# Attention kernel on one Trainium2 core: four heads of one batch per step, with the query projected in column tiles

## The chip, the cores and the metric

The kernel runs on one core of a Trainium2 chip. The metric is the device time of one execution in microseconds (us). A run is called slow when it is over 1.5% above the fastest of the same kernel, otherwise fast. Medians are of all runs on record; of the runs quoted here only one is slow, in experiment 1, and it is left out of the ratio. Ratios are the mean time of one kernel's fast runs over that of the other's in the same rounds on the same chip, so they are not quite the ratio of the medians that are quoted too.

Words used below: **PE** is TensorE's matmul row of the profile and **PEld** its weight loads; **DVE** is VectorE, **ACT** ScalarE, **POOL** GpSimd, **SP** the engine that issues the DMAs. A **step** handles four (batch, head) pairs of problem B, 128 query rows in all; there are 128 steps.

## The reference

Two attention blocks with cached keys and values, A with 4 key/value heads for 32 query heads, B with 32 for 32; their outputs stand side by side. The change touches B alone:

```python
# B, Sq, D = 16, 32, 1024;  H, Sk, Dh = 32, 1024, 128;  all bf16
q = (x @ wq).reshape(B, Sq, H, Dh).transpose(0, 2, 1, 3)
scores = einsum("bhqd,bhkd->bhqk", q, k_cache) * Dh ** -0.5
p = softmax(scores)
o = einsum("bhqk,bhkd->bhqd", p, v_cache)
return o.transpose(0, 2, 1, 3).reshape(B, Sq, H * Dh) @ wo
```

B's keys and values are 134 MB each, so the kernel is a stream of cache loads with work for every engine behind it.

## The kernel before

The program records its operations, and a list scheduler with a table of durations sets the order on each engine at build time. The parts that matter here are B's query projection, the shuffle that brings the query to where the scores need it, the key load and the scores.

```python
# projection of 128 tokens (4 batches) for 4 heads: 8 matmuls of 128x512
for j in range(j0, j0 + JS):
    last = e.matmul(ps_pj[:, 0:CW], xT_sb[:, 1, j, G * P:(G + 1) * P], wq_sb[:, 1, j, :],
                    start=(j == 0), stop=(j == DJ - 1))
# ... copied to Qtok (partition = batch, query), DVE-transposed in 32x32 blocks to QBt
# the shuffle: 16 matmuls with the identity and 4 ACT copies a group
for rg in range(4):
    last = e.matmul(QSH[0][32 * rg:32 * rg + 32, 0:2 * Dh]..., ident[32 * a:32 * a + 32, ...], rhs,
                    start=True, stop=True, tile_position=(32 * a, 32 * rg))
...
evac(QR[:, gp, a, :, :], QSH[0][:, 0:2 * Dh]..., name="QR_ev", eng="act", ...)

# keys: 2 batches x 2 heads a step, 2 runs of 16 keys (4 KB) per partition
ksrc = pb["k"][q.b0:q.b0 + 2, q.h0:q.h0 + 2].rearrange("t hh (p s) d -> (hh p) t (s d)", s=16)
pr.add("sp", lambda e: e.dma_start(KB_sb[:, sl, :, :], ksrc), ...)
# ... DVE transposes KB_sb in 32x32 blocks to KBt_sb; scores are 32 matmuls of 32x32 tiles, 512 columns;
# one exp of 1024 columns with a row sum; 4 transposes of P; 32 column-tiled matmuls with V
```

The key buffer has two slots. A slot is free for the next load when the DVE transposes have read it, and these write KBt_sb, which is free when TensorE's scores have read it.

## Time and profile before

The kernel before takes 917.8 us (median of 4 runs, 911.66 to 923.61). The profile is of one more run, of 913.31 us.

| What | Value | Where |
|---|---|---|
| hardware DMA queue busy | 97.6% | page, part 3 |
| DMA rate, mean / best slices | 375 / 409 to 411 GB/s | page, part 2 |
| PE busy | 86% | page, part 1 |
| DMA rate over 100 to 880 us | 388 GB/s | windows |

DMA is the resource that is nearly full, and TensorE follows.

The groups of instructions, kept apart by shape (busy us, mean ns | idle time of the engine before them and who ended it), show the costs that the change removes or alters.

```profile
L848 DVE STREAM_TRANSPOSE KBt_sb<-KB_sb 128x1024 f32<-128x1024 f32 x256 | 306.6, 1223 | 46.3 <-DMA KB_sb<-in_B_k_cache_dram 22.6 <-PE ps_s L887 18.9 <-PE ps_o L971 2.4
L887 PE MATMUL ps_s<-KBt_sb,QR 32*32 32x512 bf16 x4096 | 167.0, 402 | 13.8 <-ACT P_sb L907 7.4 <-DVE KBt_sb L848 4.4 <-ACT QR L588 1.2
...
L907 ACT ACTIVATE P_sb<-ps_s 128x1024 bf16<-128x1024 f32 x128 | 131.7, 1029 | 70.3 <-PE ps_pt L921 36.5 <-PE ps_s L887 28.1 <-DVE KBt_sb L848 2.0
...
L921 PE MATMUL ps_pt<-id,P_sb 128*128 128x128 f32 x512 | 91.7, 302 | 18.4 <-ACT P_sb L907 16.9 <-ACT PT_sb L588 1.3
...
L674 PE MATMUL ps_pj<-wq_sb,xT_sb 128*128 128x512 bf16 x256 | 71.0, 391 | 4.3 <-ACT QR L588 1.8 <-ACT xT_sb L588 1.2 <-DMA wq_sb<-in_B_wq_dram 0.6
...
L588 ACT CAST QR<-ps_pj 128x256 bf16<-128x256 f32 x128 | 48.5, 379 | 46.0 <-PE ps_pj L694 43.3 <-PE ps_s L887 2.6
...
L694 PE MATMUL ps_pj<-QBt,ident 32*32 32x256 bf16 x512 | 43.9, 287 | 17.5 <-ACT QR L588 10.0 <-DVE acc L748 2.6 <-DVE Qtok L590 1.5
...
```

The shuffle is L694 on PE and the QR copies on ACT. The key transposes (L848) are the biggest item on DVE; they wait 18.9 us in all for scores (L887) to free KBt_sb.

The waits of SP, which issues the loads (total us, times, longest), and the windows of the start and the middle (stretch, its length, busy us and instructions of PE, PEld, DVE, ACT and POOL, then granted clock, DMA share, GB/s):

```profile
SPq L813 <- DVE KBt_sb L848: 220.4, 64, 13.0
...
```
```profile
0.00:100.00 100.00, 77.32 (x800) 37.64 (x800) 34.88 (x56) 34.78 (x58) 6.45 (x16) 0.86 0.85 308
100.00:880.00 780.00, 687.02 (x11461) 386.27 (x11454) 472.01 (x809) 418.24 (x774) 61.38 (x59) 0.98 1.01 388
...
```

SP waits for DVE's key transposes before it can load the next keys. At 410 GB/s, the best slices, the 341.64 MB would need about 833 us by estimate; the rest is lost at the start, at the end and in such holes.

### The profile page before, as it was taken

The page shows a single profiled execution, that of the slowest core. Times are in us where ns is not written, and L with a number is a line of the kernel's source. Part 1 is how long each engine was busy: PE and PEld are TensorE (multiplying, and loading weights), DVE is VectorE, ACT ScalarE, POOL GpSimd, SP SyncE. Part 2 cuts the span into 40 slices and gives each one's busy share as a digit, 9 for nine tenths or more (in the row PEclk, how much of TensorE's full clock was granted, in tenths as well). Part 3 has the DMA queues.
Part 4 walks back from the last instruction along what each step waited for, and adds up shares of the span by engine and source line. Part 5 has one row for each costly group of instructions (what it writes and reads, how often), then busy time and mean ns, then how long its engine had stood idle before and what let it go on. Part 6 is the DMA issues. An engine that isn't in the chain of part 4 may idle for free.

```text
span 911.5 us, 28186 instructions
## 1 busy us (share of the span) xinstructions
PE 783.4 (86%) x12610; PEld 432.9 (47%) x12610; DVE 519.3 (57%) x891; ACT 462.1 (51%) x853; POOL 67.9 (7%) x76
## 2 busy tenths in 40 slices
PE   5879999999998899988898789989897888978775
PEld 2325564545554454545454455536453445545332
DVE  1415655466645566555756556666665656666553
ACT  2215665655564455655564555555554544646242
POOL 0000000100110010101010010001010100001000
PEclk7879999999999999999999999999999899989898
DMA  9789899999999999999999999999999999899995
GB/s 333 270 302 370 308 399 361 402 385 390 359 380 409 411 349 400 401 381 392 368 405 403 411 374 390 375 346 397 405 408 399 385 398 403 333 409 397 385 410 190
DMA packets 151934, 341.64 MB, mean 375 GB/s; under 512 B 10496, under 2 KB 26880, under 8 KB 151808
## 3 DMA queue, kind: packets, MB, share of 16 engines
q1 hardware_dynamic: 151808, 339.78, 97.6%
q8 instruction: 101, 1.65, 0.7%
q14 instruction: 25, 0.20, 0.1%
HBM read 337.64 MB, written 2.10 MB: 373 GB/s over the span
## 4 chain that ended last, share of the span: by engine, by line
PE 56%; ACT 14%; DVE 13%; DMA 12%; issue 2%; SPq 2%; POOL 0%; POOLq 0%; DVEq 0%; ACTq 0%
PE ps_pj L735 10%; PE ps_s L887 10%; DVE KBt_sb L848 6%; PE ps_o L971 6%; PE ps_pj L657 6%; PE ps_pt L921 6%; ACT P_sb L907 5%; PE ps_pj L674 5%; PE ps_kt L937 4%; DMA KB_sb<-in_B_k_cache_dram 4%; ACT PTA_sb L901 3%; PE ps_s L865 3%; DMA wq_sb<-in_A_wq_dram 3%; DVE acc L748 3%; PE ps_kt L839 2%
## 5 line engine op out<-in xcount | busy, mean ns | idle before, releaser
L848 DVE STREAM_TRANSPOSE KBt_sb<-KB_sb 128x1024 f32<-128x1024 f32 x256 | 306.6, 1223 | 46.3 <-DMA KB_sb<-in_B_k_cache_dram 22.6
L887 PE MATMUL ps_s<-KBt_sb,QR 32*32 32x512 bf16 x4096 | 167.0, 402 | 13.8 <-ACT P_sb L907 7.4
L901 ACT ACTIVATE PTA_sb<-ps_s 128x1024 bf16<-128x1024 f32 x128 | 131.6, 1029 | 73.1 <-PE ps_s L865 59.9
L907 ACT ACTIVATE P_sb<-ps_s 128x1024 bf16<-128x1024 f32 x128 | 131.7, 1029 | 70.3 <-PE ps_pt L921 36.5
L588 ACT COPY PT_sb<-ps_pt 128x512 f32<-128x512 f32 x128 | 74.9, 585 | 150.6 <-PE ps_o L971 116.5
L822 POOL COPY VAp_sb<-VA_sb 128x1024 bf16<-128x1024 bf16 x64 | 66.6, 1040 | 770.5 <-DMA VA_sb<-in_A_v_cache_dram 667.3
L921 PE MATMUL ps_pt<-id,P_sb 128*128 128x128 f32 x512 | 91.7, 302 | 18.4 <-ACT P_sb L907 16.9
L987 DVE TENSOR_SCALAR OB_sb<-ps_o,rinv_all 128x128 bf16<-128x128 f32 x128 | 44.4, 347 | 108.0 <-PE ps_o L971 107.6
L921 PEld LDWEIGHTS ps_pt<-id,P_sb 128*128 128x128 f32 x512 | 74.2, 208 | 43.2 <-ACT P_sb L907 25.2
L971 PE MATMUL ps_o<-VB_sb,PT_sb 128*32 128x128 bf16 x4096 | 84.9, 224 | 8.4 <-DMA VB_sb<-in_B_v_cache_dram 6.7
L865 PE MATMUL ps_s<-QT_sb,KTA_sb 128*128 128x256 bf16 x512 | 85.3, 275 | 4.2 <-ACT PTA_sb L901 2.2
L735 PE MATMUL ps_pj<-woB_sb,OTB_sb 128*128 128x512 bf16 x256 | 75.4, 391 | 12.9 <-DVE acc L748 5.4
L937 PE MATMUL ps_kt<-VAp_sb,PTA_sb 128*128 128x129 bf16 x1024 | 80.3, 221 | 5.4 <-ACT KTA_sb L588 2.3
L971 PEld LDWEIGHTS ps_o<-VB_sb,PT_sb 128*32 128x32 bf16 x4096 | 60.1, 98 | 52.1 <-issue 38.7
L657 PE MATMUL ps_pj<-xT_sb,wq_sb 128*128 128x512 bf16 x256 | 74.0, 406 | 11.4 <-DMA wq_sb<-in_A_wq_dram 4.2
L887 PEld LDWEIGHTS ps_s<-KBt_sb,QR 32*32 32x32 bf16 x4096 | 49.7, 90 | 67.5 <-issue 19.5
L937 PEld LDWEIGHTS ps_kt<-VAp_sb,PTA_sb 128*128 128x128 bf16 x1024 | 64.9, 98 | 31.2 <-issue 13.4
L674 PE MATMUL ps_pj<-wq_sb,xT_sb 128*128 128x512 bf16 x256 | 71.0, 391 | 4.3 <-ACT QR L588 1.8
L735 PE MATMUL ps_pj<-woA_sb,OTA_sb 128*128 128x512 bf16 x256 | 66.9, 389 | 7.4 <-DVE ost L751 4.7
L588 ACT CAST QR<-ps_pj 128x256 bf16<-128x256 f32 x128 | 48.5, 379 | 46.0 <-PE ps_pj L694 43.3
L748 DVE TENSOR_TENSOR acc<-acc,ps_pj 128x512 f32<-128x512 f32 x64 | 43.5, 680 | 44.6 <-PE ps_pj L735 44.2
L865 PEld LDWEIGHTS ps_s<-QT_sb,KTA_sb 128*128 128x128 bf16 x512 | 44.3, 98 | 32.3 <-ACT PTA_sb L901 5.8
(52 smaller groups left out, 574.0 us busy)
## 6 DMA issues: line engine op xcount, KB each, us to landing
KB_sb<-in_B_k_cache_dram SPq DMA_DIRECT2D x128, 1024.0 KB, 8.2
VB_sb<-in_B_v_cache_dram SPq DMA_DIRECT2D x256, 512.0 KB, 8.9
KA_sb<-in_A_k_cache_dram SPq DMA_DIRECT2D x64, 256.0 KB, 9.5
VA_sb<-in_A_v_cache_dram SPq DMA_DIRECT2D x64, 256.0 KB, 7.7
wq_sb<-in_B_wq_dram SPq DMA_DIRECT2D x32, 256.0 KB, 6.9
wq_sb<-in_A_wq_dram SPq DMA_DIRECT2D x32, 256.0 KB, 8.7
woB_sb<-in_B_wo_dram SPq DMA_DIRECT2D x32, 256.0 KB, 8.4
woA_sb<-in_A_wo_dram SPq DMA_DIRECT2D x32, 256.0 KB, 7.8
```

The costliest lines, as they stand in the source:

```text
L588: pr.add("act", lambda e: e.copy(dst_ap, src_ap), reads=reads, writes=writes, name=name + "@act", wtag=wtag, rtag=rtag)
L657: last = e.matmul(ps_pj[:, 0:tn], wq_sb[:, 0, j, hc * Dh:(hc + 1) * Dh], xT_sb[:, 0, j, t0:t0 + tn], start=(j == 0), stop=(j == DJ - 1))
L674: last = e.matmul(ps_pj[:, 0:CW], xT_sb[:, 1, j, G * P:(G + 1) * P], wq_sb[:, 1, j, :], start=(j == 0), stop=(j == DJ - 1))
L735: last = e.matmul(ps_pj[:, 0:OUTW], OT[:, gp, hh, :], wo_[:, hh, oh * OUTW:(oh + 1) * OUTW], start=(hh == 0), stop=(hh == nh - 1))
L848: pr.add("dve", lambda e: e.transpose(KBt_sb[:, sl, t_, :].bitcast(F32), KB_sb[:, rs, t_, :].bitcast(F32)), reads=[("KB", rs)], writes=[(" ...
L865: last = e.matmul(ps_s[:, sbf, c2, i * 2 * P:(i + 1) * 2 * P], KTA_sb[:, sl, c * P:(c + 1) * P], qt, start=True, stop=True)
L887: last = e.matmul(ps_s[32 * cg:32 * cg + 32, sbf, g2, :].rearrange("p (s j) -> p s j", s=16), lhsT, rhs, start=(fp == 0), stop=(fp == 3), ...
L901: pr.add("act", lambda e: e.activation(dst, src, ACTF.Exp, scale=scale), writes=BK_S[sbf] + [("PTA", q.half)], name="expA", rtag={("Sv", s ...
L907: pr.add("act", lambda e: e.activation(dst, src, ACTF.Exp, scale=scale, accum_out=stat[:, 0:1]), writes=BK_S[sbf] + ["P", "rowsum"], name= ...
L921: last = e.transpose(ps_pt32[:, m * P:(m + 1) * P], p32[:, m:Sk // 2:NPK], id32[:])
L937: last = e.matmul(ps_kt[:, qh * OA0:qh * OA0 + Dh + 1], PTA_sb[:, h, c, qh * P:(qh + 1) * P], VAp_sb[:, sl, 4 * h + c, 0:Dh + 1], start=(h ...
L971: last = e.matmul(ps_o[32 * a:32 * a + 32, 0:Dh], PT_pairs[:, c // 2, 32 * a:32 * a + 32, c % 2], VB_sb[:, kvs, a // 2, a % 2, c, :], star ...
```

## The change

A step now takes four heads of one batch. Each head gets a quadrant of 32 partitions, each partition 32 keys in one run of 8 KB. The intent is to halve the number of key packets and to have no shuffle: the projection is written so that a head's query comes out in its own quadrant, which takes column tiles of 32 columns. So that the eight matmuls of a round of scores use eight different tiles of the array, as before (there 32 of them took 1.14 us together in the timeline, where the mean of one is 402 ns), half of a head's scores land in another quadrant (`a ^ 2`); therefore the exp is cut in two, and two small DVE adds bring the halves of a row sum together.

```diff
-                ksrc = pb["k"][q.b0:q.b0 + 2, q.h0:q.h0 + 2].rearrange("t hh (p s) d -> (hh p) t (s d)", s=16)
+                ksrc = pb["k"][q.b, q.h0:q.h0 + 4].rearrange("a (p s) d -> (a p) (s d)", s=32)
 ...  (projection, per group of 128 tokens)
-                        last = e.matmul(ps_pj[:, 0:CW], xT_sb[:, 1, j, G * P:(G + 1) * P], wq_sb[:, 1, j, :], start=(j == 0), stop=(j == DJ - 1))
+            for bq in range(4):
+                    for j in range(DJ):
+                        for hh in range(4):
+                            last = e.matmul(ps_pj[32 * hh:32 * hh + 32, bq * Dh:(bq + 1) * Dh],
+                                            xT_sb[:, 1, j, G * P + 32 * bq:G * P + 32 * bq + 32], wq_sb[:, 1, j, hh * Dh:(hh + 1) * Dh],
+                                            start=(j == 0), stop=(j == DJ - 1), tile_position=(0, 32 * hh))
 ...
-        def qprepB_sh(m_, G, a_list):      # the shuffle, 16 matmuls and 4 copies a group: removed
 ...  (scores)
+                            cg = a ^ (2 * g)
+                            last = e.matmul(ps_s[32 * cg:32 * cg + 32, sbf, g, :]..., lhsT, kt[32 * a:32 * a + 32, g, :, :, o0:o0 + 63:2],
+                                            start=(fp == 0), stop=(fp == 3), tile_position=(32 * a, 32 * cg))
 ...  (exp)
+                for g in range(2):
+                    pr.add("act", lambda e, ...: e.activation(dst, src, ACTF.Exp, scale=scale, accum_out=st[:, g:g + 1]), ... name="exp", ...)
+                for i in range(2):
+                    o, r = 64 * i, 64 * (1 - i)
+                    pr.add("dve", lambda e, ...: e.tensor_tensor(st[o:o + 64, 2:3], st[o:o + 64, 0:1], st[r:r + 64, 1:2], ALU.add), ... name="shift", ...)
 ...  (the transposes of P in two halves; V by heads; output by heads)
```

More of the change, by code (lines that the diff above doesn't have):

```diff
@@ L18 @@
 LAZY_DELAY = 0
-QSH_IN_PJ = True
 A_STEPS_FRAC = 0.92
@@ L26 @@
 PRIO_BONUS = {}
-PE_MODE = {"scoresB": 2, "Qshuf": 2, "PVB": 1}
+PE_MODE = {"scoresB": 2, "PVB": 1, "qprojB": 1}
 MODE_SWITCH = 0.11
@@ L31 @@
     "scoresB": 1.1, "scoresA": 0.45, "PT_trB": 0.50, "PVB": 0.8, "OT_tr": 0.10, "KTA_tr": 0.50,
-    "Qshuf": 0.25, "qprojA": 1.8, "qprojB": 1.8, "oprojA": 1.8, "oprojB": 0.9, "xT_tr": 0.5,
-    "exp": 1.25, "expA": 1.05, "VAp_cp": 1.2, "normA@dve": 0.42, "OT_trA": 0.2, "OT_evA@dve": 0.35, "PT_ev@act": 0.52, "norm@act": 0.46, "OT_ev@act": 0.24, "KTA_ev@act": 0.93, "qA_ev@act": 0.52, "qB_ev@act": 0.52,
-    "QR_ev@act": 0.31, "acc0": 0.52, "xT_ev@act": 0.93, "o_fin@act": 0.52,
+    "qprojA": 1.8, "qprojB": 1.8, "oprojA": 1.8, "oprojB": 0.9, "xT_tr": 0.5,
+    "exp": 0.82, "shift": 0.12, "expA": 1.05, "VAp_cp": 1.2, "normA@dve": 0.42, "OT_trA": 0.2, "OT_evA@dve": 0.35, "PT_ev@act": 0.52, "norm@act": 0.46, "OT_ev@act": 0.24, "KTA_ev@act": 0.93, "qA_ev@act": 0.52, "qB_ev@act": 0.52,
+    "acc0": 0.52, "xT_ev@act": 0.93, "o_fin@act": 0.52,
     "KBt_tr": 1.15, "recip": 0.15, "norm@dve": 0.30, "PT_ev@dve": 0.62, "OT_ev@dve": 0.16, "KTA_ev@dve": 0.62,
     "QBt_tr": 0.35, "acc+": 0.62, "accF": 0.62, "qA_ev@dve": 0.62, "qB_ev@dve": 0.62, "xT_ev@dve": 0.62, "o_fin@dve": 0.62,
-    "QR_ev@dve": 0.35,
     "c0": 0.2, "c1": 0.3,
@@ L531, in build @@
         z32 = sb("z32", [P, P], F32)
-        stat = sb("stat", [P, 4], F32)
+        stat = sb("stat", [P, 2, 4], F32)
         rinv_all = sb("rinv_all", [P, 2 * NIT], F32)
@@ L540, in build @@
         Qtok = sb("Qtok", [P, 2, NG, CW], BF)
-        QBt = sb("QBt", [P, CW], BF)
-        QR = sb("QR", [P, 2, 4, 2, Dh], BF)
+        QBt = sb("QBt", [P, 2, CW], BF)
         woA_sb = sb("woA_sb", [P, HS, D], BF)
@@ L549, in build @@
         KBt_sb = sb("KBt_sb", [P, 2, 2, 16 * Dh], BF)
-        VB_sb = sb("VB_sb", [P, NVB, 2, 2, NCH, Dh], BF)
+        VB_sb = sb("VB_sb", [P, NVB, 4, NCH, Dh], BF)
         KA_sb = sb("KA_sb", [P, 2, NCH, Dh], BF)
@@ L569, in build @@
         BK_KT, BK_PT, BK_O, BK_PJ = ("bank", 4), ("bank", 5), ("bank", 6), ("bank", 7)
-        QSH = (ps_pj, BK_PJ) if QSH_IN_PJ else (ps_kt, BK_KT)
         pr.add("pool", lambda g: g.memset(zeros[:], 0.0), writes=["zeros"], name="c0")
@@ L667, in qprojB, with e_qp @@
             lazy_flush(("wq", 1, m_))
-            JS = 2 if DJ % 2 == 0 else 1
-            for j0 in range(0, DJ, JS):
-                def e_qp(e, j0=j0):
+            for bq in range(4):
+                def e_qp(e, bq=bq):
                     last = None
-                    for j in range(j0, j0 + JS):
-                        last = e.matmul(ps_pj[:, 0:CW], xT_sb[:, 1, j, G * P:(G + 1) * P], wq_sb[:, 1, j, :], start=(j == 0), stop=(j == DJ - 1))
-                    return last
-                pcs = sorted(set(j * WQP // DJ for j in range(j0, j0 + JS)))
-                pr.add("pe", e_qp, reads=[("wq", 1, k_) for k_ in pcs] + [("xT", 1, G)], writes=[BK_PJ], name="qprojB", dur=0.225 * JS,
-                       rtag=dict((("wq", 1, k_), m_) for k_ in pcs))
+                    for j in range(DJ):
[3 more added lines that the diff above has]
+                                            start=(j == 0), stop=(j == DJ - 1), tile_position=(0, 32 * hh))
+                    return last
+                pr.add("pe", e_qp, reads=[("wq", 1, k_) for k_ in range(WQP)] + [("xT", 1, G)], writes=[BK_PJ], name="qprojB", dur=0.45,
+                       rtag=dict((("wq", 1, k_), m_) for k_ in range(WQP)))
@@ L679, in qprojB, with qprepB @@
             evac(Qtok[:, m_ % 2, G, :], ps_pj[:, 0:CW], reads=[BK_PJ], writes=[BK_PJ, ("Qtok", m_ % 2, G)], name="qB_ev",
                  wtag={("Qtok", m_ % 2, G): m_})
-        def qprepB_tr(m_, G):
-            pr.add("dve", lambda e: e.transpose(QBt[:, :].bitcast(F32), Qtok[:, m_ % 2, G, :].bitcast(F32)),
-                   reads=[("Qtok", m_ % 2, G)], writes=["QBt"], name="QBt_tr", rtag={("Qtok", m_ % 2, G): m_}, wtag={"QBt": (m_, G)})
-        def qprepB_sh(m_, G, a_list):
+        def qprepB(m_, G):
@@ L687, in qprepB_sh @@
             gp = (m_ * NG + G) % 2
-            for a in a_list:
-                def e_sh(e, a=a):
-                    last = None
-                    for rg in range(4):
-                        e_ = rg // 2
-                        rhs = QBt[32 * a:32 * a + 32, :].rearrange("p (hp e x) -> p e hp x", hp=2, e=2)[:, e_, :, :]
-                        last = e.matmul(QSH[0][32 * rg:32 * rg + 32, 0:2 * Dh].rearrange("p (hp x) -> p hp x", hp=2),
-                                        ident[32 * a:32 * a + 32, 32 * a:32 * a + 32], rhs, start=True, stop=True,
-                                        tile_position=(32 * a, 32 * rg))
-                    return last
-                pr.add("pe", e_sh, reads=["QBt", "ident"], writes=[QSH[1]], name="Qshuf", rtag={"QBt": (m_, G)})
-                evac(QR[:, gp, a, :, :], QSH[0][:, 0:2 * Dh].rearrange("p (hp x) -> p hp x", hp=2), reads=[QSH[1]],
-                     writes=[QSH[1], ("QR", gp, a)], name="QR_ev", eng="act", wtag={("QR", gp, a): (m_, G)})
+            pr.add("dve", lambda e: e.transpose(QBt[:, gp, :].bitcast(F32), Qtok[:, m_ % 2, G, :].bitcast(F32)),
+                   reads=[("Qtok", m_ % 2, G)], writes=[("QBt", gp)], name="QBt_tr", rtag={("Qtok", m_ % 2, G): m_}, wtag={("QBt", gp): (m_, G)})
@@ L785, in mk_quadB @@
             q.G = (t // 4) % NG
-            jb = t % 4
-            q.bp = jb // 2
-            q.hp = jb % 2
-            q.b0 = 4 * q.G + 2 * q.bp
-            q.h0 = q.m * MS + 2 * q.hp
+            q.bq = t % 4
+            q.b = 4 * q.G + q.bq
+            q.h0 = q.m * MS
             q.kvslot = t % 2
@@ L795, in mk_quadB @@
             q.sbuf = None
-            q.first_of_group = (jb == 0)
-            q.last_of_group = (jb == 3)
+            q.first_of_group = (q.bq == 0)
+            q.last_of_group = (q.bq == 3)
             q.qid = ("B", t)
@@ L811, in st_dmaK @@
                 sl = q.krslot
-                ksrc = pb["k"][q.b0:q.b0 + 2, q.h0:q.h0 + 2].rearrange("t hh (p s) d -> (hh p) t (s d)", s=16)
-                pr.add("sp", lambda e: e.dma_start(KB_sb[:, sl, :, :], ksrc), writes=[("KB", sl)], dma_key=f"kb{sl}", name="kb_dma", dur=4 * Sk * Dh * 2, wtag={("KB", sl): q.kid})
+                ksrc = pb["k"][q.b, q.h0:q.h0 + 4].rearrange("a (p s) d -> (a p) (s d)", s=32)
+                pr.add("sp", lambda e: e.dma_start(KB_sb[:, sl, :, :].rearrange("p i n -> p (i n)"), ksrc), writes=[("KB", sl)], dma_key=f"kb{sl}", name="kb_dma", dur=4 * Sk * Dh * 2, wtag={("KB", sl): q.kid})
         def st_dmaV(q):
@@ L826, in st_dmaV @@
                 for t_ in range(2):
-                    vsrc = pb["v"][q.b0 + t_, q.h0:q.h0 + 2].rearrange("hh (p c) d -> p hh c d", c=NCH)
-                    pr.add("sp", lambda e, t_=t_, vsrc=vsrc: e.dma_start(VB_sb[:, sl, t_, :, :, :], vsrc), writes=[("VB", sl, t_)],
+                    vsrc = pb["v"][q.b, q.h0 + 2 * t_:q.h0 + 2 * t_ + 2].rearrange("a (p c) d -> p a c d", c=NCH)
+                    pr.add("sp", lambda e, t_=t_, vsrc=vsrc: e.dma_start(VB_sb[:, sl, 2 * t_:2 * t_ + 2, :, :], vsrc), writes=[("VB", sl, t_)],
                            dma_key=f"vb{sl}_{t_}", name="vb_dma", dur=2 * Sk * Dh * 2, wtag={("VB", sl, t_): q.kid})
@@ L872, in st_scores @@
                 gp = (q.m * NG + q.G) % 2
+                kt = KBt_sb[:, sl, :, :].rearrange("p i (s x) -> p (i s) x", s=16).rearrange("p (sh g cl) x -> p g sh cl x", g=2, cl=4)
                 def e_s(e, fp):
                     last = None
-                    if True:
-                        f, pd = fp // 2, fp % 2
-                        o0 = f * 64 + pd
-                        for t_ in range(2):
-                            a = 2 * q.bp + t_
-                            for hh in range(2):
-                                cg = 2 * t_ + hh
-                                for g2 in range(2):
-                                    rg = 2 * hh + g2
-                                    lhsT = QR[32 * rg:32 * rg + 32, gp, a, q.hp, o0:o0 + 63:2]
-                                    rhs = KBt_sb[32 * rg:32 * rg + 32, sl, t_, :].rearrange("p (s x) -> p s x", s=16)[:, :, o0:o0 + 63:2]
-                                    last = e.matmul(ps_s[32 * cg:32 * cg + 32, sbf, g2, :].rearrange("p (s j) -> p s j", s=16), lhsT, rhs,
-                                                    start=(fp == 0), stop=(fp == 3), tile_position=(32 * rg, 32 * cg))
+                    f, pd = fp // 2, fp % 2
+                    o0 = f * 64 + pd
+                    for a in range(4):
+                        lhsT = QBt[32 * a:32 * a + 32, gp, q.bq * Dh + o0:q.bq * Dh + o0 + 63:2]
+                        for g in range(2):
+                            cg = a ^ (2 * g)
+                            last = e.matmul(ps_s[32 * cg:32 * cg + 32, sbf, g, :].rearrange("p (sh cl j) -> p sh cl j", sh=4, cl=4), lhsT,
+                                            kt[32 * a:32 * a + 32, g, :, :, o0:o0 + 63:2],
+                                            start=(fp == 0), stop=(fp == 3), tile_position=(32 * a, 32 * cg))
@@ L889, in e_s @@
                     return last
                 for fp_ in range(4):
-                    pr.add("pe", lambda e, fp_=fp_: e_s(e, fp_), reads=[("QR", gp, 2 * q.bp), ("QR", gp, 2 * q.bp + 1), ("KBt", sl, 0), ("KBt", sl, 1)],
+                    pr.add("pe", lambda e, fp_=fp_: e_s(e, fp_), reads=[("QBt", gp), ("KBt", sl, 0), ("KBt", sl, 1)],
                            writes=BK_S[sbf], name="scoresB", dur=0.275, tag="B%d" % q.t,
-                           rtag={("QR", gp, 2 * q.bp): (q.m, q.G), ("QR", gp, 2 * q.bp + 1): (q.m, q.G), ("KBt", sl, 0): q.kid, ("KBt", sl, 1): q.kid},
+                           rtag={("QBt", gp): (q.m, q.G), ("KBt", sl, 0): q.kid, ("KBt", sl, 1): q.kid},
@@ L904, in st_exp @@
             else:
-                src = ps_s[:, sbf, :, :].rearrange("p g (s j) -> p g j s", s=16)
-                dst = P_sb[:, :].rearrange("p (g j s) -> p g j s", g=2, s=16)
-                pr.add("act", lambda e: e.activation(dst, src, ACTF.Exp, scale=scale, accum_out=stat[:, 0:1]),
-                       writes=BK_S[sbf] + ["P", "rowsum"], name="exp",
-                       rtag={("Sv", sbf): q.qid}, wtag={"P": q.qid, "rowsum": q.qid})
+                st = stat[:, q.t % 2, :]
+                for g in range(2):
+                    src = ps_s[:, sbf, g, :].rearrange("p (sh cl j) -> p j sh cl", sh=4, cl=4)
+                    dst = P_sb[:, :].rearrange("p (j sh g cl) -> p g j sh cl", sh=4, g=2, cl=4)[:, g]
+                    pr.add("act", lambda e, src=src, dst=dst, g=g: e.activation(dst, src, ACTF.Exp, scale=scale, accum_out=st[:, g:g + 1]),
+                           writes=[BK_S[sbf][g], ("P", g), ("rowsum", q.t % 2, g)], name="exp",
+                           rtag={("Sv", sbf): q.qid}, wtag={("P", g): q.qid, ("rowsum", q.t % 2, g): q.qid})
+                for i in range(2):
+                    o, r = 64 * i, 64 * (1 - i)
+                    pr.add("dve", lambda e, o=o, r=r: e.tensor_tensor(st[o:o + 64, 2:3], st[o:o + 64, 0:1], st[r:r + 64, 1:2], ALU.add),
+                           reads=[("rowsum", q.t % 2, g) for g in range(2)], writes=[("total", q.t % 2, i)], name="shift",
+                           rtag={("rowsum", q.t % 2, g): q.qid for g in range(2)}, wtag={("total", q.t % 2, i): q.qid})
         NPK = NCH // 2
@@ L916, in st_ptr, with e_pt @@
             p32 = P_sb[:, :].bitcast(F32)
-            def e_pt(e):
-                last = None
-                for m in range(NPK):
-                    last = e.transpose(ps_pt32[:, m * P:(m + 1) * P], p32[:, m:Sk // 2:NPK], id32[:])
-                return last
-            pr.add("pe", e_pt, reads=["P", "id32"], writes=[BK_PT], name="PT_trB", rtag={"P": q.qid}, wtag={"PTps": q.qid})
+            for g in range(2):
+                def e_pt(e, g=g):
+                    last = None
+                    for m in (2 * g, 2 * g + 1):
+                        last = e.transpose(ps_pt32[:, m * P:(m + 1) * P], p32[:, m:Sk // 2:NPK], id32[:])
+                    return last
+                pr.add("pe", e_pt, reads=[("P", g), "id32"], writes=[BK_PT], name="PT_trB", dur=0.25, rtag={("P", g): q.qid}, wtag={"PTps": q.qid})
         def st_pev(q, eng="act"):
@@ L970, in e_pv @@
                     for a in range(4):
-                        last = e.matmul(ps_o[32 * a:32 * a + 32, 0:Dh], PT_pairs[:, c // 2, 32 * a:32 * a + 32, c % 2], VB_sb[:, kvs, a // 2, a % 2, c, :],
+                        last = e.matmul(ps_o[32 * a:32 * a + 32, 0:Dh], PT_pairs[:, c // 2, 32 * (a ^ (c // 4 * 2)):32 * (a ^ (c // 4 * 2)) + 32, c % 2], VB_sb[:, kvs, a, c, :],
                                         start=(c == 0), stop=(c == NCH - 1), tile_position=(0, 32 * a))
@@ L978, in st_recip @@
         def st_recip(q):
-            pr.add("dve", lambda e: e.reciprocal(q.rinv, stat[:, 0:1]), reads=["rowsum"], writes=["rinv", ("rinv_all", 1)], name="recip",
-                   rtag={"rowsum": q.qid}, wtag={"rinv": q.qid})
+            pr.add("dve", lambda e: e.reciprocal(q.rinv, stat[:, q.t % 2, 2:3]), reads=[("total", q.t % 2, i) for i in range(2)], writes=["rinv", ("rinv_all", 1)], name="recip",
+                   rtag={("total", q.t % 2, i): q.qid for i in range(2)}, wtag={"rinv": q.qid})
         def st_norm(q, eng="act"):
@@ L994, in st_otr @@
             gp = (q.m * NG + q.G) % 2
-            dst = OTB_sb[:, gp, 2 * q.hp:2 * q.hp + 2, 64 * q.bp:64 * q.bp + 64].rearrange("p hh (t q) -> p t hh q", t=2)
-            evac(dst, ot_ps.rearrange("p (t hh q) -> p t hh q", t=2, hh=2), reads=[BK_O],
-                 writes=[BK_O] + [("OT", 1, gp, h_) for h_ in (2 * q.hp, 2 * q.hp + 1)], name="OT_ev", eng=eng,
+            evac(OTB_sb[:, gp, :, 32 * q.bq:32 * q.bq + 32], ot_ps.rearrange("p (a q) -> p a q", a=4), reads=[BK_O],
+                 writes=[BK_O] + [("OT", 1, gp, h_) for h_ in range(MS)], name="OT_ev", eng=eng,
                  rtag={"OTps": q.qid}, wtag={("OTv", 1, gp): (q.m, q.G)} if q.last_of_group else None)
@@ L1069, in build @@
         qprojB(0, 0)
-        qprepB_tr(0, 0)
-        qprepB_sh(0, 0, [0, 1, 2, 3])
+        qprepB(0, 0)
         for hh in range(MS):
@@ L1117, in build @@
             tn = t + (4 - t % 4)
-            if tn < NIT:
-                qn = quadsB[tn]
-                if t % 4 == 0:
-                    qprepB_tr(qn.m, qn.G)
-                qprepB_sh(qn.m, qn.G, [t % 4])
+            if tn < NIT and t % 4 == 0:
+                qprepB(quadsB[tn].m, quadsB[tn].G)
             if qB.m + 1 < NMSB:
```

## The prediction

> **What bounds it now.** DMA first, TensorE close behind. The page gives the core's hardware DMA queue 97.6% of 16 engines' time; DMA moves 341.64 MB, a mean of 375 GB/s, but the best slices show 409 to 411 GB/s. At 410 the traffic alone would need about 833 us of the 911.5 us span, so some 80 us are lost. Binned by microsecond, the trace's packets put about 25 us of loss in the first 100 us (windows view: 296 to 324 GB/s there), 48 us in 100 to 880 us (mean 388 GB/s) and 13 us in the tail. In nearly every mid-run hole the SP queue is waiting to issue a KB load: its own waits are 220 us for the DVE transposes KBt, which free the K slot; those wait in turn for TensorE's scoresB to free KBt. PE is 85 to 94% busy over 100 to 800 us, DVE about 60%, ACT about 55%.
>
> **What the change does.**
> 1. K packets go from 4096 B (32768 of them) to 8192 B (16384). Packets in the trace take a median of 46 ns at 1 KB, 84 at 2 KB, 159 at 4 KB, and 309 for the few of 8 KB (instruction queue): about 9 ns plus 37 per KB. That saves 16384 x 9 ns / 16 = 9 us of DMA time; packets overlap, so 5 to 9 us. [...]
> 2. Q shuffle goes: 43.9 us of PE busy with 17.5 us idle before it, 48.5 us of ACT (QR copies).
> 3. qprojB becomes 4096 column-tiled matmuls of 128 columns instead of 256 of 512. The 32 column-tiled PV matmuls take 0.63 us together (timeline), one alone 0.22, so about 13 ns each: 128 take 1.9 us, against 74.0/32 = 2.3 us now. Neutral.
> 4. scoresB: same count and shape, eight different tiles still; neutral (32 in 1.14 us).
> 5. exp in two halves: a 512-column ACT copy takes 585 ns against 1029 for 1024, plus a second accumulator read of 200: +0.34 us a step, +44 us ACT. With item 2, ACT is about neutral.
> 6. Two shift adds a step on DVE, estimated 0.15 us each from the tiny reciprocals (160 ns): +38 us DVE, 57% to about 61%.
>
> **How much shows.** DMA floor: -7. Start (PE-bound): -4. Mid-run holes: with PE below 85% the K slot comes free earlier; I take a bit under half of 48 us: -18 (an estimate: a list scheduler reorders everything). Against a profiled 911.5 that is about 883; against the median 919.76 and allowing for an untuned order I say 895 us, 80% range 872 to 917. Chances: faster by over 2% 0.62, within 2% 0.32, slower 0.06.
>
> **What would show it.** KB loads made of 16384 packets of 8192 B with median near 309 ns; no Qshuf, no QR; PE about 730 to 745 us; qprojB 65 to 90 us; scoresB about 165; exp near 585 x256; DVE about 555; DMA mid-run above 392 GB/s; SP's wait on KBt transposes smaller.
>
> **What would make it wrong.** The hardware cuts 8 KB runs into 4 KB packets (then -7 is lost). Holes come from the fixed order or DVE's in-order waits on the later exp half, not from PE load: then only about -10 (within 2%). New tile order serialises scoresB tiles of one row group: PE +50 us and slower. Shorter runs in exp slow ACT.

## More of the kernel before

From the page of the kernel before: the busy times of the engines with their instruction counts, the DMA queues (packets, MB, share), and the engines' shares of the chain that ended last.

```profile
span 911.5 us, 28186 instructions
...
PE 783.4 (86%) x12610; PEld 432.9 (47%) x12610; DVE 519.3 (57%) x891; ACT 462.1 (51%) x853; POOL 67.9 (7%) x76
...
q1 hardware_dynamic: 151808, 339.78, 97.6%
q8 instruction: 101, 1.65, 0.7%
...
PE 56%; ACT 14%; DVE 13%; DMA 12%; issue 2%; SPq 2%; POOL 0%; POOLq 0%; DVEq 0%; ACTq 0%
...
```

In the chain (the work that ended last, followed back step by step to what released it), only 2% is "issue", time in which an engine waited for nothing that the profile shows. Queue q8 carries instructions: 101 packets.

## The result, and the profile after

The changed kernel takes 983.36 us (median of 4 runs, 978.79 to 985.89). The ratio of its fast runs to those of the kernel before is 1.071, with a 95% interval of 1.0625 to 1.0795. It is slower by 7%, outside the predicted range and on its other side. Its result is correct.

The same lines of the page, after:

```profile
span 980.0 us, 35212 instructions
...
PE 788.4 (80%) x15938; PEld 474.0 (48%) x15938; DVE 561.0 (57%) x1147; ACT 447.5 (46%) x981; POOL 68.1 (7%) x76
...
q1 hardware_dynamic: 135424, 339.78, 91.4%
q8 instruction: 126, 2.06, 0.8%
...
PE 55%; DVE 21%; issue 9%; ACT 7%; DMA 5%; SPq 2%; DVEq 0%; POOLq 0%
...
```

DMA is now at 91.4%, PE at 80%: everything is less busy, so something holds TensorE or DMA up without working. The chain names it: "issue" rose from 2% to 9%, about 70 us of 980 more, about as much as the kernel lost. The instruction queue rose from 101 packets to 126. PE has 15938 matmuls and as many weight loads, against 12610 of each.

The groups after:

```profile
L828 DVE STREAM_TRANSPOSE KBt_sb<-KB_sb 128x1024 f32<-128x1024 f32 x256 | 305.6, 1224 | 60.4 <-PE ps_s L864 53.0 <-DMA KB_sb<-in_B_k_cache_dram 5.0 <-PE ps_o L977 1.6
L864 PE MATMUL ps_s<-KBt_sb,QBt 32*32 32x512 bf16 x4096 | 162.8, 398 | 34.4 <-issue 18.7 <-DVE KBt_sb L828 6.5 <-ACT P_sb L887 6.4
L887 ACT ACTIVATE P_sb<-ps_s 128x512 bf16<-128x512 f32 x256 | 151.7, 598 | 88.1 <-PE ps_s L864 47.9 <-PE ps_pt L906 39.1
...
L906 PE MATMUL ps_pt<-id,P_sb 128*128 128x128 f32 x512 | 109.1, 314 | 13.2 <-ACT PT_sb L584 5.2 <-ACT P_sb L887 3.8 <-issue 3.1
...
L670 PE MATMUL ps_pj<-wq_sb,xT_sb 128*32 128x128 bf16 x4096 | 75.2, 227 | 33.6 <-issue 21.9 <-DMA wq_sb<-in_B_wq_dram 5.5 <-DVE acc L730 2.1
...
L892 DVE TENSOR_TENSOR stat<-stat 64x1 f32<-64x1 f32 x256 | 41.9, 164 | 45.6 <-ACT P_sb L887 38.3
...
```

The busy times are near what was predicted: the projection (L670) 75.2 us against 71.0, scores the same, a half exp 598 ns, a shift add (L892) 164 ns. Only the transposes of P (L906) grew much, from 91.7 to 109.1 us. But look at the idle times. The projection and the scores now wait for "issue", and the key transposes wait 53.0 us for scores, 18.9 before. The three largest waits of PE, first before, then after, as total us, times, longest:

```profile
PE ps_pt L921 <- ACT P_sb L907: 16.9, 22, 1.4
PE ps_pj L694 <- ACT QR L588: 10.0, 21, 1.2
PE ps_s L887 <- ACT P_sb L907: 7.4, 11, 1.4
...
```
```profile
PE ps_pj L670 <- issue: 21.9, 13, 3.5
PE ps_s L864 <- issue: 18.7, 8, 4.5
PE ps_o L956 <- issue: 18.1, 11, 4.3
...
```

One such wait in the timeline of the changed kernel (start us, us, engine, line):

```profile
...
205.81 1.79 PEld L670 LDWEIGHTS ps_pj<-wq_sb,xT_sb 128*32 128x32 bf16 x128 [1.17 <-ACT QT_sb L584]
205.81 1.97 PE L670 MATMUL ps_pj<-wq_sb,xT_sb 128*32 128x128 bf16 x128 [0.68 <-ACT QT_sb L584]
...
207.56 0.32 PEld L956 LDWEIGHTS ps_o<-VB_sb,PT_sb 128*32 128x32 bf16 x17
207.61 0.40 PE L956 MATMUL ps_o<-VB_sb,PT_sb 128*32 128x128 bf16 x16
...
212.31 0.29 PE L956 MATMUL ps_o<-VB_sb,PT_sb 128*32 128x128 bf16 x8 [4.31 <-issue]
212.31 0.12 PEld L956 LDWEIGHTS ps_o<-VB_sb,PT_sb 128*32 128x32 bf16 x7 [4.44 <-issue]
...
```

A column-tiled projection runs: 128 loads and 128 matmuls in 1.97 us. The matmuls with V follow. After 17 loads and 16 matmuls, between a load and its own matmul, TensorE stops and does nothing for 4.31 us. The profile shows nothing that it waits for ("issue").

The trace also has every DMA packet, and the packets of the instruction queue q8 are 16384 B long. Their number goes with TensorE's instructions (loads, matmuls, its recorded waits and four others): 101 packets for 25514 in the kernel before, 126 for 32144 in the changed one, about one for every 256. Counting these instructions from the start gives a sharp answer:

- In the changed kernel the gaps of PE and PEld together that lie just ahead of instruction 193 + 256k (counting from 0), for whole k, sum to 71.2 us. (The 193 was read off the trace; it is the same in the other forms that stop.) The gaps at any other position in the 256 sum to 0.4 us on average, 3.7 us at most.
- 33 of these 125 boundaries have a gap of over 0.5 us. Before every one of them exactly k instruction packets have landed, and in 32 of the 33 TensorE goes on 1.2 to 1.6 us after the landing of the k-th. In the example, that packet ran from 210.08 to 211.00 us.
- In the kernel before, the same positions hold 0.4 us of gaps.

A **block** here is the 256 instructions between two of these boundaries. The author reads the stops as TensorE having run out of instructions; what is measured is where they stand and when they end. The k-th packet starts a median of 3.5 us after the boundary before the k-th (2.9 us in the kernel before) and takes 0.94 us, and where TensorE had stopped it goes on some 1.4 us after the landing. The three medians add up to some 5.8 us, an estimate with a wide spread, so a stop would be expected after most blocks that are used up much faster. So it is: 28 of the 33 blocks that were used up in under 5 us ended in a gap of over 0.5 us, and 5 of the 91 others. Here is how long the 256 instructions took, without the gap after them:

| Time in which a block was used up | Blocks before | Blocks after | of these with a gap over 0.5 us | their gaps, us |
|---|---|---|---|---|
| under 4 us | 0 | 22 | 20 | 53.8 |
| 4 to 5 us | 0 | 11 | 8 | 10.9 |
| 5 to 6 us | 2 | 13 | 2 | 2.4 |
| over 6 us | 96 | 78 | 3 | 4.1 |

One projection call is 256 instructions in 1.97 us, as many as a whole block. All 33 short blocks hold at least 82 instructions of the projection.

What the stops do to the rest can be followed back through the lines. Scores come late; KBt_sb is freed late; the key transposes wait (53.0 us); the key slot is freed late; SP waits longer for it and DMA stands idle. The waits of SP and the windows after:

```profile
SPq L793 <- DVE KBt_sb L828: 186.2, 44, 14.1
SPq L793 <- DVE stat L892: 157.9, 41, 9.5
...
```
```profile
0.00:100.00 100.00, 66.73 (x1377) 41.01 (x1378) 32.92 (x58) 28.79 (x53) 5.43 (x15) 0.90 0.78 283
100.00:880.00 780.00, 647.49 (x13245) 393.69 (x13243) 467.92 (x961) 376.62 (x824) 59.42 (x57) 0.96 0.95 359
...
```

The key load (L793) depends on the key transposes alone; "stat" is a small DVE instruction that the view took for the releaser because it came last. Taken together, the waits of the key load for DVE in the lines of that view rose from 334 to 500 us, and the rate over 100 to 880 us fell from 388 to 359 GB/s.

### The profile page after: what moved, and what is told of

It is laid out like the page before. It is cut to its first block, busy times and chain, and to the rows that moved or that the text cites. A ratio compares the mean times of both kernels' runs of the same rounds, so it can differ in the third digit from the quotient of the medians.

```text
span 980.0 us, 35212 instructions
## 1 busy us (share of the span) xinstructions
PE 788.4 (80%) x15938; PEld 474.0 (48%) x15938; DVE 561.0 (57%) x1147; ACT 447.5 (46%) x981; POOL 68.1 (7%) x76
## 3 DMA queue, kind: packets, MB, share of 16 engines
q1 hardware_dynamic: 135424, 339.78, 91.4%
## 4 chain that ended last, share of the span: by engine, by line
PE 55%; DVE 21%; issue 9%; ACT 7%; DMA 5%; SPq 2%; DVEq 0%; POOLq 0%
DVE KBt_sb L828 13%; PE ps_s L864 11%; PE ps_pj L717 8%; PE ps_pj L670 6%; PE ps_pt L906 6%; PE ps_kt L922 6%; PE ps_pj L653 5%; PE ps_o L956 5%; PE ps_s L845 4%; ACT P_sb L887 3%; DVE acc L730 2%; PE ps_kt L819 2%; DMA KB_sb<-in_B_k_cache_dram 2%; ACT PTA_sb L879 2%; DMA wq_sb<-in_B_wq_dram 1%
## 5 line engine op out<-in xcount | busy, mean ns | idle before, releaser
L887 ACT ACTIVATE P_sb<-ps_s 128x512 bf16<-128x512 f32 x256 | 151.7, 598 | 88.1 <-PE ps_s L864 47.9
L864 PE MATMUL ps_s<-KBt_sb,QBt 32*32 32x512 bf16 x4096 | 162.8, 398 | 34.4 <-issue 18.7
L906 PE MATMUL ps_pt<-id,P_sb 128*128 128x128 f32 x512 | 109.1, 314 | 13.2 <-ACT PT_sb L584 5.2
L956 PE MATMUL ps_o<-VB_sb,PT_sb 128*32 128x128 bf16 x4096 | 92.0, 228 | 22.1 <-issue 18.1
L670 PE MATMUL ps_pj<-wq_sb,xT_sb 128*32 128x128 bf16 x4096 | 75.2, 227 | 33.6 <-issue 21.9
L906 PEld LDWEIGHTS ps_pt<-id,P_sb 128*128 128x128 f32 x512 | 80.9, 207 | 39.6 <-ACT PT_sb L584 16.9
L845 PE MATMUL ps_s<-QT_sb,KTA_sb 128*128 128x256 bf16 x512 | 91.7, 284 | 8.3 <-ACT PTA_sb L879 4.8
L864 PEld LDWEIGHTS ps_s<-KBt_sb,QBt 32*32 32x32 bf16 x4096 | 48.0, 90 | 98.8 <-issue 45.8
L670 PEld LDWEIGHTS ps_pj<-wq_sb,xT_sb 128*32 128x32 bf16 x4096 | 63.0, 101 | 46.3 <-issue 33.8
L892 DVE TENSOR_TENSOR stat<-stat 64x1 f32<-64x1 f32 x256 | 41.9, 164 | 45.6 <-ACT P_sb L887 38.3
```

The costliest lines, as they stand in the source:

```text
L670: last = e.matmul(ps_pj[32 * hh:32 * hh + 32, bq * Dh:(bq + 1) * Dh], xT_sb[:, 1, j, G * P + 32 * bq:G * P + 32 * bq + 32], wq_sb[:, 1, j, ...
L845: last = e.matmul(ps_s[:, sbf, c2, i * 2 * P:(i + 1) * 2 * P], KTA_sb[:, sl, c * P:(c + 1) * P], qt, start=True, stop=True)
L864: last = e.matmul(ps_s[32 * cg:32 * cg + 32, sbf, g, :].rearrange("p (sh cl j) -> p sh cl j", sh=4, cl=4), lhsT, kt[32 * a:32 * a + 32, g, ...
L887: pr.add("act", lambda e, src=src, dst=dst, g=g: e.activation(dst, src, ACTF.Exp, scale=scale, accum_out=st[:, g:g + 1]), writes=[BK_S[sbf ...
L906: last = e.transpose(ps_pt32[:, m * P:(m + 1) * P], p32[:, m:Sk // 2:NPK], id32[:])
L956: last = e.matmul(ps_o[32 * a:32 * a + 32, 0:Dh], PT_pairs[:, c // 2, 32 * (a ^ (c // 4 * 2)):32 * (a ^ (c // 4 * 2)) + 32, c % 2], VB_sb[ ...
```

## The experiments

Theory 1 was the one above: bursts of small TensorE instructions use up a block before the next packet of the instruction queue has landed, and TensorE stops. Theory 2 was that the half exps, the shift adds and the longer DVE chain slow the pipeline, and that the gaps are only a symptom. Theory 3 was that column tiling itself is slow.

### 1 and 2. The kernel before, with its projection cut into column tiles

The layout, the result and the order of operations are those of the kernel before (compared instruction by instruction); only the projection is written in more, smaller matmuls. W = 128 gives 128 matmuls a call, W = 512 gives 32 with the same column tiles.

```diff
-                        last = e.matmul(ps_pj[:, 0:CW], xT_sb[:, 1, j, G * P:(G + 1) * P], wq_sb[:, 1, j, :], start=(j == 0), stop=(j == DJ - 1))
+                        for c0 in range(0, CW, W):
+                            for bq in range(4):
+                                last = e.matmul(ps_pj[32 * bq:32 * bq + 32, c0:c0 + W], xT_sb[:, 1, j, G * P + 32 * bq:G * P + 32 * bq + 32],
+                                                wq_sb[:, 1, j, c0:c0 + W], start=(j == 0 and c0 == 0), stop=(j == DJ - 1),
+                                                tile_position=(0, 32 * bq), skip_group_check=True)
```

> The kernel before, its instruction order unchanged, with the B projection alone written as 128 column-tiled matmuls of 128 columns a call instead of 8 of 512 (same layout, same result). Theory 1 (TensorE runs out of instructions: 3840 more matmuls and as many weight loads, about 30 more instruction blocks of 256, burned off 256 in about 2 us a call): 960 to 1010 us, with PE gaps at exact multiples of 256 instructions summing to over 50 us, against 4.5 us in the kernel before. Theory 2 (the loss comes from the half exps, the shift adds and the longer DVE chain): within 1% of the kernel before. Theory 3 (column tiling itself[...]): slower too, but then also in the 32-matmul form.

> As the 128 form, but 32 column-tiled matmuls of 512 columns a call: the same column tiles[...] with a quarter of the instructions (768 more matmuls, 6 more blocks). Theory 1: within 1.5% of the kernel before, block gaps under 15 us. Theory 2: within 1%. Theory 3: about as slow as the 128 form, 960 us or more.

(The blocks of 256 are the spacing of the stops in the changed kernel, and the 2 us are the 1.97 us of its timeline. The 4.5 us in the first text is the largest sum at any position of the 256 in the kernel before, at 173; at 193, the position of the stops, it is 0.4 us.)

Measured: the 128 form took 1001.78 us (ratio 1.0878, 1.0808 to 1.0949), with block gaps of 56.2 us in 33 places. One of its four runs, of 1006.59 us, was slow. The 32 form took 930.0 us (1.0168, 1.0133 to 1.0203), with 2.1 us. The pages of the 128 form and the 32 form, busy times, instruction queue and chain:

```profile
...
PE 824.7 (82%) x16450; PEld 485.7 (49%) x16450; DVE 519.7 (52%) x891; ACT 463.9 (46%) x853; POOL 67.9 (7%) x76
...
q8 instruction: 130, 2.13, 0.8%
...
PE 62%; ACT 14%; DVE 10%; issue 7%; DMA 5%; SPq 1%; POOLq 0%; DVEq 0%; ACTq 0%
...
```
```profile
...
PE 794.6 (86%) x13378; PEld 430.2 (47%) x13378; DVE 518.8 (56%) x891; ACT 462.8 (50%) x853; POOL 67.9 (7%) x76
...
q8 instruction: 106, 1.74, 0.7%
...
PE 60%; ACT 15%; DVE 12%; DMA 8%; issue 2%; SPq 1%; POOL 0%; POOLq 0%; DVEq 0%; ACTq 0%
...
```

This part of the change alone costs more than the whole change, in a kernel with the old layout, one exp and no shift adds. Theory 2 does not explain it. The 32 form has the same column tiles at the same places in the order and costs 1.7%, a little over the 1.5% that was expected, so theory 3 has at most that share (PE busy rose by 11 us). Between the two forms lie 72 us: 54 us of block gaps, and 30 us more PE busy. Part of the latter may be the clock. The granted clock of the profiled run was 0.944 in the 128 form and 0.971 in the 32 form, and matmuls that the edit does not touch took longer (scores 412 ns for 404, A's scores 281 for 274, products with B's V 230 for 225). An estimate from the two clocks, 2.8% of 794.6 us, is some 22 us. How much of it counts was not taken apart.

### 3. The dose between them

W = 256 in the same edit gives 64 matmuls a call, half a block.

> Dose between the two: the kernel before, order unchanged, B projection as 64 column-tiled matmuls of 256 columns a call. Theory 1 (a block of 256 TensorE instructions that is used up in under about 5 us outruns the fetch of the next): a call now takes half a block, so few blocks fall under 5 us: block gaps 5 to 25 us and 930 to 955 us, between 930 (32 form) and 1002 (128 form) and nearer the former. If the cost were simply proportional to instructions it would be about 950 to 957.

Measured: 932.57 us (1.0194, 1.0136 to 1.0251), block gaps 6.7 us. The cost is not proportional to the number of instructions: 1536 to 2048 more instructions than the next smaller form cost 14.5 and 2.6 us, the last 4096 cost 69 us (medians from two rounds on different chips; the ratios, 1.017, 1.019 and 1.088, say the same), and only in the last form do many blocks pass in under 5 us (1, 4 and 30 blocks in the three forms). The 5 us of the expectation is from the table of the changed kernel: 28 of 33 blocks below it were followed by a stop, 5 of 91 above.

### 4. The same instructions, spread out

The changed kernel with the same TensorE instructions in another order. The four quarters of a projection call start at least 2.5 us apart in the scheduler, except in the first block of heads.

```diff
+PROJ_SPACING = 2.5
 ...
                 r = op.t1 + (0.0 if same_pe else lat)
+                if op.name == "qprojBs" and uo.name == "qprojBs":
+                    r = op.t0 + PROJ_SPACING
```

> The changed kernel with the same TensorE instructions, but after the first block of heads the four quarters of a column-tiled projection are scheduled at least 2.5 us apart (109 bursts of mostly 32 matmuls instead of 58 of up to 128). Theory 1: bursts, not the sum of instructions, starve TensorE: block gaps fall from 71 us to 20 to 45 us and the time to 925 to 965 us. If only the total number of instructions counts: gaps stay above 60 us and the time above 970 us.

Measured: 950.96 us (1.0414, 1.034 to 1.0489), 32 us less than the changed kernel with the same instructions (some 27 us by the two ratios, as the rounds differ). The gaps fell only to 51.4 us, so that half of the expectation failed; "issue" is still 8% of the chain. Still 33 blocks pass in under 5 us, but 10 of them in under 4 us where it was 22: the quarters now stand among scores and matmuls with V, which are also small instructions. The direction supports bursts rather than the sum. The time fell by more than the gaps did (20 us), so another part of the gain came from the new order, which this run cannot separate.

### 5. The change without the burst, shuffle by TensorE

The changed kernel with the full-width projection back. Four matmuls and one copy for each batch exchange the quadrants, as the kernel before did with wider ones.

```diff
-  128 column-tiled matmuls a call (as in the change)
+  last = e.matmul(ps_pj[:, 0:CW], xT_sb[:, 1, j, G * P:(G + 1) * P], wq_sb[:, 1, j, :], start=(j == 0), stop=(j == DJ - 1))
 ...
+  for hh in range(4):   # for each batch bq, after the DVE transpose to Qmv
+      last = e.matmul(ps_pj[32 * hh:32 * hh + 32, 0:Dh], ident[32 * bq:32 * bq + 32, 32 * bq:32 * bq + 32],
+                      Qmv[32 * bq:32 * bq + 32, hh * Dh:(hh + 1) * Dh], start=True, stop=True, tile_position=(32 * bq, 32 * hh))
+  evac(QBt[:, gp, bq * Dh:(bq + 1) * Dh], ps_pj[:, 0:Dh], ..., name="QR_ev", eng="act", ...)
```

> The changed kernel with the B projection full-width again (8 matmuls of 512 a call) and the quadrants exchanged by 16 small matmuls and 4 copies a group, as the kernel before did: 8 KB keys, half exps and shift adds stay, TensorE's instruction count is that of the kernel before. Theory 1: block gaps under 10 us, time 890 to 925 us. Theory 2: still 955 us or more.

Measured: 917.68 us (1.0037, 1.0001 to 1.0072), block gaps 5.6 us. From its page:

```profile
...
PE 778.2 (85%) x12610; PEld 435.2 (48%) x12610; DVE 563.2 (62%) x1147; ACT 471.6 (52%) x1109; POOL 67.9 (7%) x76
...
q8 instruction: 100, 1.64, 0.6%
...
PE 45%; DVE 20%; DMA 18%; ACT 10%; issue 3%; SPq 2%; POOL 0%; DVEq 0%; POOLq 0%
...
```

The 8 KB keys, the half exps and the shift adds are all still there, and the loss is gone. This settles against theory 2. It also shows that without the burst, but with a shuffle, the new layout gains nothing.

### 6. The change without the burst, shuffle by GpSimd

POOL is busy 7% of the time. The projection is the full-width one of experiment 5. Here POOL's 16 copies of 32x128 a group, 287 ns each in the mean of 512, exchange the quadrants, one after the other and in series with all its other work.

```diff
+            for bq in range(4):
+                for hh in range(4):
+                    pr.add("pool", lambda g, ...: g.tensor_copy(Qmv[32 * hh:32 * hh + 32, bq * Dh:(bq + 1) * Dh],
+                                                                Qtok[32 * bq:32 * bq + 32, m_ % 2, G, hh * Dh:(hh + 1) * Dh]),
+                           reads=[("Qtok", m_ % 2, G)], writes=["Qmv", "poolser"], name="Qmv", dur=0.25, ...)
-            ... e.transpose(QBt[:, gp, :].bitcast(F32), Qtok[:, m_ % 2, G, :].bitcast(F32))
+            ... e.transpose(QBt[:, gp, :].bitcast(F32), Qmv[:, :].bitcast(F32))
```

> The changed kernel with the B projection full-width and the quadrants exchanged by 16 copies a group on the otherwise idle GpSimd: fewest TensorE instructions of all (12098 matmuls). Theory 1: block gaps under 10 us, 880 to 915 us, perhaps faster than both kernels. Theory 2: still 955 us or more. Own risk: GpSimd's copies delay its copies of A's values.

> The GpSimd version once more, unchanged, with more rounds: 0.975 to 0.986 of the kernel before. It also tells whether the 4 KB form (0.989) and the doubled shift adds (0.993) are really slower than it: expected, by 0.5 to 1.5%.

Measured: 899.63 us (0.9803, 0.9747 to 0.9859), and in the repetition 899.71 us (0.9852, 0.9796 to 0.9907). It is correct, faster than the kernel before by 1.5 to 2%, and so faster than both; both intervals lie below 1, but not clear of a 2% line. The page, with the same lines as above, and the middle window:

```profile
span 901.1 us, 28065 instructions
...
PE 760.1 (84%) x12098; PEld 426.2 (47%) x12098; DVE 568.2 (63%) x1147; ACT 446.8 (50%) x981; POOL 214.8 (24%) x588
...
q1 hardware_dynamic: 135424, 339.78, 97.8%
q8 instruction: 96, 1.57, 0.6%
...
PE 46%; DVE 21%; DMA 16%; ACT 9%; issue 4%; SPq 2%; POOL 1%; DVEq 0%; POOLq 0%
...
```
```profile
100.00:880.00 780.00, 671.81 (x11096) 381.68 (x11093) 517.26 (x1047) 406.77 (x899) 194.49 (x524) 0.98 1.01 393
...
```

DMA is back at 97.8%, the middle at 393 GB/s, the instruction queue at 96 packets, and block gaps sum to 2.4 us. It is 18 us faster than the form with TensorE's shuffle, where PE is 18 us and ACT 25 us busier. The form has the time that was predicted for the change (895 us, 872 to 917), but not all of its reasons: PE is at 760.1 us, not at 730 to 745, and 388 to 393 GB/s over 780 us is worth some 10 us by estimate, not 18.

### 7 and 8. Two terms of the prediction by themselves

In the GpSimd form, the key load is cut in two DMAs, so that packets are 4 KB again:

```diff
-                ksrc = pb["k"][q.b, q.h0:q.h0 + 4].rearrange("a (p s) d -> (a p) (s d)", s=32)
+                ksrc = pb["k"][q.b, q.h0:q.h0 + 4].rearrange("a (p i s) d -> i (a p) (s d)", i=2, s=16)
+                for i_ in range(2):
+                    pr.add("sp", lambda e, i_=i_: e.dma_start(KB_sb[:, sl, i_, :], ksrc[i_]), writes=[("KB", sl, i_)], ...)
```

> The GpSimd version with each key load cut in two DMAs, so that key packets are 4096 B again and nothing else differs. If the packet saving of the prediction is right: 0.5 to 1.2% slower than the GpSimd version (899.6 us), so 904 to 911 us. If 8 KB packets are worth nothing because other waits set the pace: within 0.3% of it.

Measured: 906.65 us (0.9894, 0.9852 to 0.9936), 7 us over the GpSimd form's medians. The rounds were others, on another chip. By the ratios it is 0.4% (against the repetition) to 0.9% slower, about 4 to 8 us. Its interval overlaps with both of the GpSimd form, so the saving is likely rather than shown, and the form has one more DMA a step as well.

And the shift adds done twice, the copies into a spare column:

```diff
+                    pr.add("dve", lambda e, o=o, r=r: e.tensor_tensor(st[o:o + 64, 3:4], st[o:o + 64, 0:1], st[r:r + 64, 1:2], ALU.add),
+                           reads=[("rowsum", q.t % 2, g) for g in range(2)], writes=[("spare", q.t % 2, i)], name="shift", ...)
```

> The GpSimd version with the two shift adds of a step done twice (the copies go to a spare column that nothing reads): about 45 us more work on DVE. If DVE is off the limit, as the prediction took it: within 0.5% of the GpSimd version (899.6 us). If its in-order waits on the second exp hold up the key transposes: 1% or more slower, 909 us or over.

Measured: 909.89 us (0.9929, 0.9885 to 0.9974), 10 us over the GpSimd form's medians (0.8 to 1.3% by the ratios, about 7 to 11 us), for 41 us more DVE busy time (608.8 against 568.2). The prediction had counted no time for more work on DVE; about a quarter of added DVE work seems to show. This interval is clear of the first one of the GpSimd form but overlaps with that of its repetition, so this too is likely rather than sure. The repetition was expected to show both forms slower by 0.5 to 1.5%: the doubled adds are within that, the 4 KB form just under it.

### 9. Measured durations in the scheduler

The GpSimd form with four entries of the duration table set to the durations in its trace ("exp" 0.80, "shift" 0.19, "KBt_tr" 1.22, GpSimd copy 0.29).

> The GpSimd version with four durations of the scheduler's model set to those measured in its own trace (half exp 0.80 us, shift add 0.19, key transpose 1.22, GpSimd copy 0.29). Only the order of instructions changes. Expected: within 1% of the GpSimd version either way; faster would mean that part of the remaining loss is the order.

Measured: 903.99 us (0.9886, 0.9833 to 0.9939), 4 us over the GpSimd form of the same rounds, with intervals that overlap. Truer durations gave no better order.

The gaps at block boundaries beside the times of all forms that bear on the cause:

| Kernel | Matmuls | Blocks used up in under 5 us | Gaps at block boundaries, us | Median time, us |
|---|---|---|---|---|
| before | 12610 | 0 | 0.4 | 917.8 |
| before, 32 a call | 13378 | 1 | 2.1 | 930.0 |
| before, 64 a call | 14402 | 4 | 6.7 | 932.6 |
| before, 128 a call | 16450 | 30 | 56.2 | 1001.8 |
| changed | 15938 | 33 | 71.2 | 983.4 |
| changed, spread | 15938 | 33 | 51.4 | 951.0 |
| changed, TensorE shuffle | 12610 | 0 | 5.6 | 917.7 |
| changed, GpSimd shuffle | 12098 | 0 | 2.4 | 899.6 |

## Why the prediction was wrong

The step that failed is item 3: "128 take 1.9 us, against 74.0/32 = 2.3 us now. Neutral." The 1.9 us was right (1.97 us in the timeline), and so was the busy time, 75.2 us in the range of 65 to 90. The conclusion was not. (The 74.0 is the busy time of A's projection; B's own was 71.0, which makes 2.2 us and changes nothing.) The step counted the time of the array and not the instructions: 256 in 2 us instead of 16. That used up a whole block in 1.97 us, where the next packet started a median of 3.5 us after a boundary. The stops were 71.2 us, 70.8 us more than before, and the kernel lost 65.6 us between the medians. That the two are so close is partly chance: the GpSimd form, which keeps the rest of the change, is 84 us faster than the changed kernel with 69 us less of gaps, and the 128 form lost 86 us with 56 us of gaps. The prediction named four ways of being wrong, and this was none of them. (Of those on the hardware, the packets stayed whole at 8192 B, the scores in the new tile order took 162.8 us for 167.0, and a half exp took 598 ns where 585 was expected; the "+50 us" was a guess, with no trace behind it.)

Point by point:

- DMA is the limit and PE close behind: right. When PE stopped, holes in DMA grew as the chain of slots says, from 388 to 359 GB/s.
- 8 KB packets save 5 to 9 us: the packets came as 8192 B with a median of 309 ns, as predicted. Their value was 4 to 8 us in experiment 7, not clear of noise. In the traces a packet's time is not quite in proportion to its size: 318 ns for two packets of 4 KB (159 each), 309 for one of 8 KB. That packets overlap shows in the DMA share of 1.01 in the middle of the kernel before.
- The shuffle's removal frees PE: the 43.9 us went, but PE did not fall to 730 to 745 us; it was 788.4. The transposes of P, issued in two halves, grew from 91.7 to 109.1 us, which the prediction had not costed, and three groups that the change hardly touches (both products with V, A's scores) grew by 6 to 7 us each. The removal is worth something only when nothing costlier takes its place: in the GpSimd form PE is at 760.1 us and the kernel 18 us faster than with a TensorE shuffle.
- Scores neutral: right (162.8 against 167.0 us). ACT about neutral: right (447.5 against 462.1 us).
- DVE about 555 us: right (561.0). That this costs no time, as its sum had it: likely wrong; 41 us more cost some 7 to 11 us in experiment 8. In the changed kernel DVE stood idle for 38.3 us before the shift adds, waiting for the exp (L892).
- The holes shrink by 18 us: wrong in the changed kernel, where they grew. In the GpSimd form the middle rose from 388 to 393 GB/s.

What stays open: why an instruction packet starts 3.5 us after a boundary, and whether the data packets hold it up. The traces point that way. In the changed kernel, at the 12 boundaries where data packets filled less than 70% of the DMA engines' time in the next 3 us, the median start was 1.1 us after the boundary; at the 101 where they filled over 90%, it was 3.5 us (in the 128 form, 1.1 us at 16 and 3.5 us at 104). This goes together but is not shown to be the cause: no run took the data away. The 18 us of the 72 between the 32 and the 128 form that are not block gaps, and the part of the spread form's gain beyond its gaps, were not separated either. The granted clock was mostly lower in the two forms with the longest stops in all: 0.935 to 0.947 in the runs of the changed kernel and 0.940 to 0.957 in those of the 128 form, against 0.949 to 0.981 in the fast runs of the kernel before in the experiments' rounds. Why, and what it cost, is open. It does not make the gaps, which are idle time. Nor does it set the order of the forms: the GpSimd form (0.957 to 0.974) is faster than the one with TensorE's shuffle (0.968 to 0.983).

## What to carry to other kernels

Cost small matmuls by instructions as well as by array time: a load and a matmul are two, and in the changed kernel 28 of the 33 blocks of 256 TensorE instructions that were used up in under 5 us were followed by a stop, of up to 4.5 us. "Issue" waits in the middle of a group of one operation, at a spacing of 256 instructions, were the mark of it here (71.2 us of gaps there, 0.4 us before); compare the packets of the instruction queue before and after a change (101 and 126 here). When an operand has to move between quadrants, an idle engine may do it with no TensorE instruction at all, as GpSimd did here (12098 matmuls for 12610, and 18 us less than with TensorE's shuffle).
